# Long convolution with soft mixture of experts: x loaded in two blocks of 64 and 32 rows

## The chip, the cores and the metric

The kernel runs on one core of a Trainium2 chip. The metric is the device time of one execution in microseconds (us). TensorE is PE in the profile, VectorE DVE, ScalarE ACT, GpSimd POOL, and SyncE, which issues nearly all DMAs, SP.

## The reference, cut to what matters

`x` is (8, 5696, 128) and `h` is (5696, 128), both float32. Each of the 8 batches is convolved with `h` along its 5696 tokens, causally and per channel, by a transform of double length. The 45568 tokens that result go through a soft mixture of experts with 8 experts of 4 slots.

```python
Xf = np.fft.rfft(x, n=2*S, axis=1); Hf = np.fft.rfft(h, n=2*S, axis=0)
y = np.fft.irfft(Xf * Hf[None], n=2*S, axis=1)[:, :S, :]
t = y.reshape(B * S, D)
logits = t @ phi                       # 32 slots
slot_input = softmax(logits, over tokens).T @ t
slot_out = relu(slot_input @ w1) @ w2  # for each expert
out = softmax(logits, over slots) @ slot_out
```

## The kernel before, in words

The transform is a two-level one with N1 = 90 and N2 = 64. A sequence of 5696 tokens is seen as R1 = 89 rows of 64 tokens (5696 = 89 * 64; the transform along the rows yields 90 values). There are nine sequences ("batches" g): g = 0 is `h`, and g = 1 to 8 are the batches of `x`. A sequence is cut into NJ = 8 pieces of CH = 4 columns and their mirror images, so there are 72 steps t, one for each piece.

Stage A, once for each step. `load_x` brings piece c into one of three buffers `xc` of shape 128 partitions x 2 x 4 x 128: a row of x goes to a partition, and of each row two runs of 4 x 128 floats (2,048 bytes each) are taken, the piece and its mirror image. In the last piece of a sequence the two runs touch, and are one run of 4,096 bytes. `load_x(t + 3)` is called in step t, so a load is three steps ahead of its use. `fold` (L200, on POOL) adds and subtracts the two halves into `x0` and `x1`. `stage_a` multiplies them from the left by the table `s1` (L211, 128 x 128 weights, K = 128 partitions always), copies the bank to `fst` on ACT (L213) and stores the result in the DRAM tensor `f` by two DMAs of 45 partitions (L217), one from partition F0 = 6 and one from F1 = 82.

The 89 rows stand at partitions X0 = 20 to 108. They are loaded by two DMAs, rows 0 to 79 (SPLIT = 80) to partitions 20 to 99, and rows 80 to 88 to partitions 100 to 108. The remaining partitions of `xc` hold the zeros that a memset left there at the start, and the rows of `s1` that belong to them are zero too.

Stage B (`load_g` L230, `stage_b1` L244, `stage_b2` L284) reads `f` back in units of 128 partitions (`gt`, five buffers, asked for four units ahead), transforms along the other direction, multiplies by the transform of `h`, transforms back and stores in the DRAM tensor `z` (L289). It runs nine steps behind stage A, 23 units for each sequence. Stage C (`load_pair` L319, `stage_c1` to `stage_c6`) reads `z` back into `zc`, finishes the inverse transform and does the token side of the mixture of experts. Its load is already in the form that the change gives to x: 64 rows at partition 32 and 26 rows at partition 0, each row 16,384 bytes (`z_blocks`). There is such a pair of loads in every second step from t = 25 on.

The order of the program is written out by hand in the loop from L558. On SP's queue a step reads: the f stores and gt loads of the first half, `load_pair` (every second step), `load_x(t + 3)`, the two f stores of `stage_a(t, 1)`, a gt load, a z store. So the two x loads stand just behind the large `zc` loads, and just ahead of an f store and a gt load. All of them are in one queue. The last part of the program (from step 72) holds no x loads: the rest of stages B and C, the experts, and the output.

Of the kernel before, what the change touches and what calls it, by code (L numbers as in the profile page):

```python
# [17 lines left out]
def z_blocks(n):  # L18

    return [(0, 64, 32), (64, n - 64, 0)]  # L20


def transform_tables(S, N1, N2, CH, X0, F0, F1):

    N, R1, HALF, P = N1 * N2, S // N2, N2 // 2, 2 * N2
    k1 = np.arange(N1)
    alpha = np.pi * (k1 + 0.5) / N1
    m1 = np.arange(R1) - (N1 - 1) / 2
    a1 = np.outer(m1, alpha)  # L40
    s1 = np.stack([np.cos(a1), -np.sin(a1), -np.cos(a1)], 1)
    a0 = np.outer(alpha, np.arange(N1 // 2) + 0.5)
    i1 = np.stack([np.cos(a0), -np.sin(a0), -np.cos(a0)], 1)
    NP = N1 // 2
    part = s1
    s1 = np.zeros((P, 3, P))
    for a, p in enumerate((F0, F1)):
        s1[X0:X0 + R1, :, p:p + NP] = part[:, :, a * NP:(a + 1) * NP]
    part = i1[np.arange(N1).reshape(2, NP).T.reshape(-1)]
    i1 = np.zeros((P, 3, N2))  # L50
    for r, n, p in z_blocks(N1):
        i1[p:p + n, :, 0:NP] = part[r:r + n]
    k2 = np.arange(N2)
    omega = np.pi * (k1[:, None] + 2 * N1 * k2[None] + 0.5) / N
    m2 = np.arange(HALF) - (N2 - 1) / 2
    a2 = m2[None, :, None] * omega[:, None, :]
    w = np.concatenate([np.cos(a2), np.sin(a2)], 1)
    back = np.arange(N2).reshape(2, HALF // CH, CH).transpose(1, 0, 2).reshape(-1)
    NU = (NP + 1) // 2
    turn = (N1 - 1) / 2 * alpha[:, None] + (N2 - 1) / 2 * omega  # L60
    wq = np.zeros((2, N2, NP, N2))
    vq = np.zeros((2, N2, NU, 2, N2))
    tn = np.zeros((2, N2, 2, NU, 2))
    for a in range(2):
        wq[a] = w[a * NP:(a + 1) * NP].transpose(1, 0, 2)
        for q in range(NP):
            vq[q % 2, :, q // 2, a] = w[a * NP + q][back].T
            tn[q % 2, :, 0, q // 2, a] = np.cos(turn[a * NP + q]) / N
            tn[q % 2, :, 1, q // 2, a] = np.sin(turn[a * NP + q]) / N
    wq, vq, tn = [t.reshape(P, *t.shape[2:]) for t in (wq, vq, tn)]  # L70
    return [np.ascontiguousarray(t, dtype=np.float32) for t in (s1, i1, wq, vq, tn)]
# [3 lines left out]
def kernel(  # L75
# [26 lines left out]
    B, S, D = x.shape  # L102
# [4 lines left out]
    N1, N2 = 90, 64  # L107
    R1, HALF, NP = S // N2, N2 // 2, N1 // 2
    CH = 4
# [5 lines left out]
    HP = P // 2  # L115
    NQ = NJ // 2
    assert S == R1 * N2 and R1 == N1 - 1 and D == P and CH == Q == 4
    SPLIT = R1 // 16 * 16
    X0, F0, F1 = 20, 6, 82
    ctx.enter_context(tc.manual_schedule())  # L120

    t_s1, t_i1, t_w, t_v, t_turn = [
        nc.inline_tensor(t, f"tab_{n}").ap()
        for n, t in zip(("s1", "i1", "w", "v", "turn"), transform_tables(S, N1, N2, CH, X0, F0, F1))]
    fd = [nc.dram_tensor(f"f_{g}", (2, N2, NP, 2, D), F32, kind="Internal").ap() for g in range(B + 1)]
    zd = [nc.dram_tensor(f"z_{b}", (NP, 2 * N2, 2, D), F32, kind="Internal").ap() for b in range(B)]
    cd = nc.dram_tensor("c_t", (P, B * NQ, Q, 2, MH), F32, kind="Internal").ap()
# [7 lines left out]
    i1 = const.tile([P, 3, HP], F32, name="i1")  # L135
# [24 lines left out]
    s1 = apool.tile([P, 3, P], F32, name="s1", tag="s1", bufs=1)  # L160
    wt = fconst.tile([P, NP, HP], F32, name="wt")
    vt = fconst.tile([P, NU, 2, HP], F32, name="vt")
    turn = fconst.tile([P, 2, NU, 2], F32, name="turn")
# [3 lines left out]
    def bank():  # L167
        rings.append(rings.pop(0))
        return rings[-1].tile([P, 512], F32, name="bank", tag="bank")
# [8 lines left out]
    def load_x(c):  # L178
        if c >= (B + 1) * NJ:
            return  # L180
        g, j = divmod(c, NJ)
        src = (h if g == 0 else x[g - 1]).rearrange("(a n) d -> a n d", n=N2)
        t_ = xcs[c % len(xcs)]
        gap = N2 - CH * (2 * j + 1)
        for r in (slice(0, SPLIT), slice(SPLIT, R1)):
            v = src[r, CH * j:CH * (j + 1), :]
            v = bass.AP(tensor=v.tensor, offset=v.offset,
                        ap=[v.ap[0], [gap * D, 2], [1, CH * D]])
            nc.sync.dma_start(
                out=t_[X0 + r.start:X0 + r.stop, :, :, :].rearrange("p s n d -> p s (n d)"), in_=v)  # L190
        xs[c] = t_

    folded = {}
# [349 lines left out]
    loaded = 0  # L543

    load_x(0)
    nc.scalar.dma_start(out=s1[:, :, :], in_=t_s1)
    for c in range(1, 3):
        load_x(c)
# [9 lines left out]
    for t in range(last_front + 1):  # L558
# [73 lines left out]
        if t >= NA - 1:  # L632
# [6 lines left out]
            for r in (slice(N1 - 64, 32), slice(96, P)):  # L639
                nc.sync.dma_start(  # L640
                    out=zn[r, :, :, :, :, :].rearrange("k h o n c d -> k (h o n c d)"),
                    in_=zring[0][r, :, :, :, :, :].rearrange("k h o n c d -> k (h o n c d)"))
# [21 lines left out]
        if pair(-2) is not None:  # L664
            load_pair(pair(-2))
        load_x(t + 3)
        if t == NJ:
            prefetch(AHEAD)
# [38 lines left out]
    for q in range(Q):  # L707
        r = slice(q * NSL, (q + 1) * NSL)
        nc.gpsimd.tensor_copy(out=rep4[r, :, :],
                              in_=ident[r, r].unsqueeze(1).broadcast_to([NSL, Q, NSL]))  # L710
# [16 lines left out]
    for V in range(T, NT - 1):  # L727
# [33 lines left out]
        if V == T:  # L761
# [4 lines left out]
                              in_=moe_w1[E // 2:].rearrange("e d f -> d e f"))  # L766
        else:
            for i in range(4 * (V - T - 1), min(4 * (V - T), E), 2):
                nc.sync.dma_start(
                    out=w2s[:, i:i + 2, :, :],  # L770
                    in_=moe_w2[i:i + 2].rearrange("e (p c) d -> p e c d", p=P))
# [5 lines left out]
    p = bank()  # L777
# [8 lines left out]
    p = bank()  # L786
# [18 lines left out]
    for g in range(EG):  # L805
        for f0 in range(0, F, FH):
            p = bank()
# [4 lines left out]
            src = p[:, :].rearrange("p (c k) -> p k c", k=NFC)  # L812
# [4 lines left out]
    for g in range(EG):  # L817
        for k0 in range(0, NFC, 4):
            p = bank()
            for k in range(4):  # L820
# [3 lines left out]
                out=hidT[:, g, k0:k0 + 4, :], in_=p[:, :].rearrange("p (k c) -> p k c", k=4))  # L824
# [11 lines left out]
    p = bank()  # L836
# [20 lines left out]
    for b in range(B):  # L857
        first = [(0, 8), (8, 24)] if b == 0 else [(0, 32)]
        for r0, rows in first + [(32, 32), (64, 24)]:
# [3 lines left out]
            parts, at, r = [], 0, r0  # L863
            for n in (32, 16, 8):
                if rows & n:
                    parts.append((at, n * W // P, r))
                    at, r = at + n * W // P, r + n
# [14 lines left out]
            for q in range(Q):  # L882
                dst = ov4[:, 0:used + lone, q, :]
                src = pq[q][:, 0:(used + lone) * D].rearrange("p (k d) -> p k d", d=D)
# [4 lines left out]
            for at, n, r in parts:  # L889
                nc.sync.dma_start(  # L890
                    out=ov[b, r * N2:(r + n * P // W) * N2, :].rearrange(
                        "(p n) d -> p (n d)", p=P),
                    in_=o_[:, at * Q:(at + n) * Q, :].rearrange("p n d -> p (n d)"))
            if lone:
                nc.sync.dma_start(
                    out=ov[:, (R1 - 1) * N2:, :].rearrange("b (j n) d -> b j (n d)", n=CH),
                    in_=o_[:, used * Q:(used + 1) * Q, :].rearrange("p q d -> p (q d)"))
# [31 lines left out]
```

## Time and profile before

| what | value |
|---|---|
| median of 11 runs (range) | 925.08 us (920.18 to 935.58) |
| the profiled execution's own time | 926.8 us |
| its span, first to last instruction | 924.6 us |
| mean granted clock of TensorE | 0.961 |
| PE, DVE, ACT, POOL busy | 91%, 71%, 55%, 52% |
| DMA packets of SP's queue (q1), and MB | 164,795, 271.39 MB |
| x loads (with those of h) | 72 of 320 KB and 72 of 36 KB |
| zc loads | 28 of 1,024 KB and 28 of 416 KB |

Busy times are shares of the span. "DMA share" is the mean busy share of the core's 16 DMA engines. In the list of waits a line reads: who waited, for whom, us in total, how often, the longest. In the chain and the timeline a line begins with its start and its length in us.

### The profile page before, as it was taken

The numbers are of one execution on the slowest core, as the hardware profiler recorded it, in microseconds if no ns is written. First come the engines' busy times: TensorE is split into PE (matmuls) and PEld (weight loads), VectorE is DVE, ScalarE is ACT, GpSimd is POOL, SyncE is SP. The second block draws the span as 40 slices with busy tenths as digits, with TensorE's granted clock in tenths as the row PEclk, the third lists the DMA queues.
The fourth block names the chain that finished last, engine by engine and source line by source line (L and its number), as shares of the span: only waits on it lengthen the run. The fifth ranks groups of instructions, "written<-read, shape, count | busy, mean of one in ns | idle before, by whom it ended". The sixth has DMA issues, their size and how long they took to land.

```text
span 924.6 us, 20380 instructions
## 1 busy us (share of the span) xinstructions
PE 837.6 (91%) x7220; PEld 402.6 (44%) x7220; DVE 656.3 (71%) x1119; ACT 512.0 (55%) x1018; POOL 476.7 (52%) x437
## 2 busy tenths in 40 slices
PE   6968888889999999999999999999998888897994
PEld 2323233334444444444444444444443334354894
DVE  3035576678888887887788788878886888786443
ACT  3546545446666665665565656565664454676442
POOL 4647623335565555555455555555545567575300
PEclk9989999999999999999999999999998999998955
DMA  8889899999999999999999999999998788885897
GB/s 287 268 269 279 267 286 330 295 322 307 313 301 315 298 298 296 329 307 275 306 277 300 296 304 299 293 297 303 323 334 249 244 282 268 256 292 186 322 419 321
DMA packets 165471, 273.04 MB, mean 295 GB/s; under 512 B 14886, under 2 KB 117542, under 8 KB 160277
## 3 DMA queue, kind: packets, MB, share of 16 engines
q1 hardware_dynamic: 164795, 271.39, 91.7%
q8 instruction: 58, 0.95, 0.4%
q10 hardware_dynamic: 576, 0.36, 0.2%
q14 instruction: 42, 0.34, 0.1%
HBM read 142.85 MB, written 128.21 MB: 293 GB/s over the span
## 4 chain that ended last, share of the span: by engine, by line
PE 63%; DMA 20%; DVE 4%; ACT 4%; POOL 3%; issue 3%; SPq 2%; DVEq 0%; ACTq 0%; POOLq 0%
PE bank L211 19%; PE bank L336 11%; PE bt L244 11%; DMA gt<-f 9%; PE bz L284 7%; DMA f<-fst 6%; DMA out_dram<-o 3%; PE bank L370 3%; PE bank L455 2%; PE op L873 2%; PE bank L379 2%; PE bank L408 2%; POOL y L360 2%; PE bank L431 2%; ACT fst L213 1%
## 5 line engine op out<-in xcount | busy, mean ns | idle before, releaser
L211 PE MATMUL bank<-x,s 128*128 128x512 f32 x576 | 284.1, 620 | 10.8 <-POOL x L200 8.3
L200 POOL TENSOR_TENSOR x<-xc 128x512 f32<-128x512 f32 x144 | 183.4, 1275 | 146.8 <-PE bank L211 98.2
L213 ACT ACTIVATE fst<-bank 128x512 f32<-128x512 f32 x288 | 167.6, 596 | 96.8 <-PE bank L211 67.0
L265 DVE TENSOR_TENSOR pr<-bt,Hr 128x512 f32<-128x512 f32 (+1 forms) x184 | 126.9, 689 | 108.5 <-PE bt L244 98.1
L288 ACT ACTIVATE zst<-bz 128x512 f32<-128x512 f32 (+1 forms) x184 | 108.2, 588 | 149.9 <-PE bz L284 143.3
L244 PE MATMUL bt<-gt,wt 64*64 64x256 f32 x1620 | 138.8, 406 | 47.8 <-DMA gt<-f 21.3
L211 PEld LDWEIGHTS bank<-x,s 128*128 128x128 f32 x576 | 99.8, 192 | 133.6 <-issue 88.5
L270 DVE TENSOR_TENSOR yf<-pr,pi 128x512 f32<-128x512 f32 (+1 forms) x166 | 145.1, 874 | 5.7
L268 DVE TENSOR_TENSOR pi<-bt,Hi 128x512 f32<-128x512 f32 (+1 forms) x184 | 125.0, 680 | 0.0
L284 PE MATMUL bz<-yf,vt 64*64 64x256 f32 x1440 | 116.2, 382 | 2.0 <-DVE yf L270 0.6
L244 PEld LDWEIGHTS bt<-gt,wt 64*64 64x64 f32 x1620 | 45.4, 133 | 164.7 <-PE bank L211 41.7
L336 PE MATMUL bank<-zc,i 128*64 128x512 f32 x448 | 110.9, 618 | 0.0
L360 POOL TENSOR_TENSOR y<-y,op 128x512 f32<-128x512 f32 x64 | 77.4, 1210 | 58.9 <-DVE op L341 56.3
L360 POOL TENSOR_TENSOR y<-y,om 128x512 f32<-128x512 f32 x59 | 82.1, 1391 | 2.1
L284 PEld LDWEIGHTS bz<-yf,vt 64*64 64x64 f32 x1440 | 52.6, 132 | 38.3 <-issue 12.7
L255 DVE SCALAR_TENSOR_TENSOR Hr<-bt,turn,ph 128x128 f32<-128x128 f32 (+1 forms) x46 | 16.0, 349 | 69.7 <-ACT ph L253 69.7
L370 PE MATMUL bank<-ident,y 109*128 109x109 f32 x512 | 57.2, 262 | 3.0 <-POOL y L360 3.0
L372 ACT ACTIVATE yt<-bank 128x360 f32<-128x360 f32 x128 | 52.1, 473 | 12.5 <-PE bank L370 12.4
L370 PEld LDWEIGHTS bank<-ident,y 109*128 109x128 f32 x512 | 48.6, 141 | 18.2 <-issue 11.6
L444 POOL TENSOR_TENSOR L<-L,rs 128x512 f32<-128x512 f32 x32 | 43.0, 1344 | 16.6 <-DVE rs L443 13.0
L873 PE MATMUL op<-so,cT 32*128 32x128 f32 x704 | 48.5, 413 | 2.8 <-ACT o L888 2.2
L336 PEld LDWEIGHTS bank<-zc,i 128*64 128x64 f32 x448 | 27.9, 139 | 50.5 <-issue 45.4
(100 smaller groups left out, 867.1 us busy)
## 6 DMA issues: line engine op xcount, KB each, us to landing
f<-fst SPq DMA_DIRECT2D x288, 180.0 KB
gt<-f SPq DMA_DIRECT2D x198, 256.0 KB
z<-zst SPq DMA_DIRECT2D x176, 256.0 KB
zc<-z SPq DMA_DIRECT2D x28, 1024.0 KB
xc<-in_x_dram SPq DMA_DIRECT2D x64, 320.0 KB
out_dram<-o SPq DMA_DIRECT2D x15, 1024.0 KB
zc<-z SPq DMA_DIRECT2D x28, 416.0 KB
out_dram<-o SPq DMA_DIRECT2D x9, 512.0 KB
```

Of the source, the lines that this page charges most:

```text
L200: nc.gpsimd.tensor_tensor(out=y_[:, :, :], in0=t_[:, 0, :, :], in1=t_[:, 1, ::-1, :], op=AL.subtract if comp else AL.add)
L211: nc.tensor.matmul(p[:, :], s1[:, tab[G], :], src[:, :, :].rearrange("p n d -> p (n d)"), start=True, stop=True)
L213: nc.scalar.activation(st[:, :, G, :], p[:, :].rearrange("p (n d) -> p n d", d=D), AF.Copy)
L244: nc.tensor.matmul(bt[q * HP:(q + 1) * HP, a, 0:2 * D], wt[r, 2 * i + q, :], t_[r, q, :, :].rearrange("p c d -> p (c d)"), start=True, sto ...
L265: nc.vector.tensor_tensor(out=pr[r, :, :, :], in0=pv, in1=Hr[r, i, :, :].unsqueeze(2).broadcast_to([n * HP, 2, 2, D]), op=AL.mult)
L268: nc.vector.tensor_tensor(out=pi[r, :, :, :], in0=pv, in1=Hi[r, i, :, :, :], op=AL.mult)
L270: adder.tensor_tensor(out=y_[r, :, :, :], in0=pr[r, :, :, :], in1=pi[r, :, ::-1, :], op=AL.add)
L284: nc.tensor.matmul(bz[a * HP:(a + 1) * HP, q, 0:2 * D], vt[r, i, a, :], y_[r, a, :, :].rearrange("p c d -> p (c d)"), start=True, stop=True)
L288: nc.scalar.activation(st[:, 0:n, :], bz[:, 0:n, 0:2 * D], AF.Copy)
L336: nc.tensor.matmul(p[h_ * HP:(h_ + 1) * HP, :], i1[:, tab, :], t_[:, h_, o, :, q, :], start=True, stop=True)
L360: eng.tensor_tensor(out=part(v, f), in0=part(v, 0), in1=o_[:, :, :], op=sign)
L370: nc.tensor.transpose(p[:, i * TR:(i + 1) * TR], ys[T][0:TR, k * CH + i, 0:D], ident[0:TR, 0:TR])
```

## The change

The 89 rows are loaded as rows 0 to 63 to partitions 32 to 95, and rows 57 to 88 to partitions 0 to 31. Rows 57 to 63 are thus loaded twice. The table `s1` gets its rows at the same places: rows 0 to 63 at partition 32, rows 64 to 88 at partitions 7 to 31, and zeros at partitions 0 to 6, where the repeated rows lie, and at 96 to 127. Nothing else in the program is different: the number of instructions, their order on each engine and their shapes are the same but for the shapes of the x loads.

```diff
+def x_blocks(n):
+    return [(0, 64, 32), (n - 32, 32, 0)]
...
     for a, p in enumerate((F0, F1)):
-        s1[X0:X0 + R1, :, p:p + NP] = part[:, :, a * NP:(a + 1) * NP]
+        done = 0
+        for r, n, row in x_blocks(R1):
+            s1[row + done - r:row + n, :, p:p + NP] = part[done:r + n, :, a * NP:(a + 1) * NP]
+            done = r + n
...
-    SPLIT = R1 // 16 * 16
-    X0, F0, F1 = 20, 6, 82
+    F0, F1 = 6, 82
...
-        for r in (slice(0, SPLIT), slice(SPLIT, R1)):
-            v = src[r, CH * j:CH * (j + 1), :]
+        for r, n, p in x_blocks(R1):
+            v = src[r:r + n, CH * j:CH * (j + 1), :]
             v = bass.AP(tensor=v.tensor, offset=v.offset,
                         ap=[v.ap[0], [gap * D, 2], [1, CH * D]])
             nc.sync.dma_start(
-                out=t_[X0 + r.start:X0 + r.stop, :, :, :].rearrange("p s n d -> p s (n d)"), in_=v)
+                out=t_[p:p + n, :, :, :].rearrange("p s n d -> p s (n d)"), in_=v)
```

More of the change, by code (lines that the diff above doesn't have):

```diff
@@ L20, in z_blocks, with transform_tables @@
     return [(0, 64, 32), (64, n - 64, 0)]
-def transform_tables(S, N1, N2, CH, X0, F0, F1):
+def x_blocks(n):
+    return [(0, 64, 32), (n - 32, 32, 0)]
+def transform_tables(S, N1, N2, CH, F0, F1):
     N, R1, HALF, P = N1 * N2, S // N2, N2 // 2, 2 * N2
@@ L123 @@
         nc.inline_tensor(t, f"tab_{n}").ap()
-        for n, t in zip(("s1", "i1", "w", "v", "turn"), transform_tables(S, N1, N2, CH, X0, F0, F1))]
+        for n, t in zip(("s1", "i1", "w", "v", "turn"), transform_tables(S, N1, N2, CH, F0, F1))]
     fd = [nc.dram_tensor(f"f_{g}", (2, N2, NP, 2, D), F32, kind="Internal").ap() for g in range(B + 1)]
```

## The prediction

> **What bounds the kernel now.** I read the page first, for the busy shares and the chain.
>
> ```profile
> PE 837.6 (91%) x7220; PEld 402.6 (44%) x7220; DVE 656.3 (71%) x1119; ACT 512.0 (55%) x1018; POOL 476.7 (52%) x437
> ...
> q1 hardware_dynamic: 164795, 271.39, 91.7%
> ...
> PE 63%; DMA 20%; DVE 4%; ACT 4%; POOL 3%; issue 3%; SPq 2%; DVEq 0%; ACTq 0%; POOLq 0%
> ```
>
> PE and the 16 DMA engines are both busy for 91% or more, so a change to the DMAs alone could matter or vanish. The split by stage decides (columns: PE, PEld, DVE, ACT, POOL busy, granted clock, DMA share, GB/s):
>
> ```profile
> 45.00:185.00 140.00, 114.48 (x737) 42.94 (x736) 79.78 (x171) 74.09 (x146) 64.46 (x60) 0.96 0.93 287
> 185.00:700.00 515.00, 501.94 (x4260) 231.34 (x4260) 420.32 (x680) 309.00 (x598) 284.03 (x245) 1.00 0.97 303
> ```
>
> From 185 to 700 us, where 44 of the 72 x loads fall (the first at 181.8), PE is idle for 13.1 of 515 us although DMA has 97%. Whatever DMA gains there, the end cannot gain over 13.1 us; a loss has no such cap. Then the waits of that stretch, PE's and SP's, and POOL's waits for x over the whole run:
>
> ```profile
> PE bt L244 <- DMA gt<-f: 11.5, 8, 2.5
> ...
> SPq L217 <- DMA zc<-z: 98.8, 39, 5.0
> SPq L230 <- DMA f<-fst: 18.0, 6, 4.4
> ...
> SPq L230 <- DMA xc<-in_x_dram: 9.8, 24, 0.8
> ```
> ```profile
>   DMA xc<-in_x_dram: 6.5, 4
> ```
>
> x itself is hardly waited for: fold L200 lost 6.5 us in four waits, being fed three steps ahead. (SP's waits for zc and x come from its eight DMA semaphores, used in turn: a ninth DMA waits until the first has landed.) PE waits for gt, in eight places. One of them, by the chain and then by PE's timeline:
>
> ```profile
> 336.79 8.62 DMA f<-fst
> ...
> 345.49 2.84 DMA gt<-f
> ```
> ```profile
> 348.38 0.66 PE L244 MATMUL bt<-gt,wt 64*64 64x256 f32 x8 [0.59 <-DMA gt<-f]
> ```
>
> An f store that usually lands 4.5 us after its issue (its median, from the semaphore updates) took 8.6, and the gt load behind it 2.8; other matmuls covered all but 0.59 us. The stretch before it shows why it was late:
>
> ```profile
> 337.00:338.00 1.00, 1.00 (x22) 0.51 (x24) 1.00 (x2) 0.74 (x2) 1.00 (x2) 1.00 0.88 344
> ...
> 339.00:340.00 1.00, 1.00 (x17) 0.61 (x10) 0.94 (x4) 0.33 (x1) 1.00 (x2) 1.00 0.70 139
> 340.00:341.00 1.00, 1.00 (x14) 1.00 (x13) 0.96 (x2) 1.00 (x4) 1.00 (x1) 1.00 0.73 141
> 341.00:342.00 1.00, 1.00 (x13) 0.81 (x15) 0.74 (x1) 1.00 (x4) 1.00 (x2) 1.00 1.06 260
> ```
>
> A `zc` pair was issued at 333.5 us, x behind it at 334.7. While the 64-row zc block moves, the rate is 344 GB/s; when the 26-row block at partition 0 and x move, it falls to 140. The packet records say the same: 16 KB packets that begin in the fourth microsecond after the issue took 687 ns on average, in the sixth and seventh 1,200; 2,048-byte packets there took 164 to 173 ns against a median of 84 over the run. Of the x loads, 22 stand behind a zc pair; their 80-row DMA lands 9.8 us after issue (median), in the other steps 4.9.
>
> **The change part by part.**
>
> *Instructions.* SP issues two x DMAs a step before and after, in the same place (their issue takes 0.42 us each, median). Nothing passes another queue, no wait is added, and POOL, PE, ACT and DVE run the same instructions on 128 partitions: `s1` has K = 128 either way, and the zeros are weights. Cost: 0.
>
> *Rows on a DMA engine.* How many engines a DMA uses is seen in the semaphore updates that it leaves: 16 for the 80 rows, ten for the nine rows (nine engines and one step of the issuer), and the 4-byte completion packets in q1 (14,566) are what the largest divisor of the row count up to 16 gives for every DMA. So nine engines carried 5 + 1 rows, seven carried 5; after, 64 and 32 rows make 4 + 2 on all. The fullest engine has 12 packets of 2,048 bytes in both: 12 x 84 ns = 1.01 us. The seven lighter ones gain two packets, 0.17 us. That the fullest engines end a load is visible: the nine-row DMA lands 0.18 to 0.20 us (two packets) after the 80-row one in 47 of 61 pairs. In the other 14 a lighter engine is last, and there the pair may come up to 0.17 us later, in a load that is three steps early. Cost on the path: 0.
>
> *Bytes.* Seven more rows are 28,672 bytes a load, 72 loads: q1 should show 2.06 MB more (273.5), 0.76%. At the stage's 303 GB/s that is 0.095 us a load, at the 141 GB/s of the slow stretch 0.203. All 72 loads fully exposed would be 6.8 us at the first rate. But only eight gt waits in this stretch reach PE. In them, with x ahead in the queue at the slow rate: 8 x 0.203 = 1.6 us. In the other steps it is hidden by PE's own work; without that cover the 22 slow loads cost 4.5 us. From 45 to 185 us PE idles 25.5 us, but 7.7 us of that is gt, in three waits, while the f and x loads run beside no zc load: up to 3 x 0.095 = 0.3, which I leave out.
>
> *Placement.* No row shows a 64-row x load at partition 32 or a 32-row one at partition 0; the nearest are the two zc blocks at the same partitions. Good end: x in 64 rows moves as the 64-row zc block does, at full speed even there. Ten packets at 160 ns become eight at 84 (-0.93 us), two at 160 become four (+0.32): -0.6 us. Bad end: the 32 rows go as the 26-row block does. 128 KB at 140 GB/s is 0.94 us where 36 KB took 0.26 (+0.68), less 64 KB at 340 GB/s (-0.19): +0.5 us. Outside the slow stretches x packets take 94 to 99 ns on average beside 84, so there is nothing to win, and any loss has PE's cover. Between -0.6 and +0.5 I take 0: each block is nearest to its own zc row, and the two ends nearly cancel.
>
> [...]
>
> *Sum.* The profiled execution took 926.8 us (span 924.6), 1.7 above the median of 925.1. From the median: 925.1 + 1.6 = 926.7.
>
> **The rivals.**
>
> *Slower: the low block becomes the bottleneck.* 16 engines write 32 low partitions just behind 13 engines that write 26 of the same. The bad end, 0.5 us plus 0.2 for the bytes, in 8 stretches (5.6) to 22 (15, if every slow stretch then reaches PE): 931 to 940, likeliest 932. For it: the 140 GB/s rows. Against it: the fullest engine has no more rows. It decides from 0.58 us a place on in eight places, or 0.21 in 22 (4.6 us).
>
> *Faster: x was slow through its own placement.* 0.6 us less in 8 stretches (-4.8), and SP's 9.8 us of waiting for x to land before it issues gt shrink as well; the cap is the 11.5 us that PE waits there for gt: 914 to 920, likeliest 919. For it: the 80 rows straddle both halves of the partitions, and rate falls when they move. Against it: in 39 loads without a zc pair ahead the same 80 rows run at 94 to 99 ns.
>
> *The rows aren't the matter:* the waits of 9.8 us behind zc are zc's own 1,440 KB, and x, at 356 KB, moves nothing. That is my forecast without the 1.6 us: 925.
>
> **How the numbers follow.** A measurement of this kernel can tell about 0.5% (4.6 us) from no change. Forecast (925 to 928, with or without the bytes): 0.41. Slower rival: 0.38, since loss has no cap and three things point there (bytes, low partitions, seven engines more at work). Faster rival: 0.21, since it needs more than a third of all PE idleness of the stage. The forecast's own range is 921 to 929.7. For 8 in 10 the range reaches to 917 and 936, leaving out the far end of each rival.
>
> **What would show it.** q1 with 273.5 MB and about 1,450 packets more (945 of data, 504 of completion) shows the bytes and the 16 engines. The gt wait of PE from 185 to 700 us tells the cases apart: 11 to 14 us for the forecast, over 16 for the slower rival, under 7 for the faster. In the slow stretches the mean of the 2,048-byte packets should stay at 150 to 170 ns; near 100 it is the faster rival, near 200 the slower. PE's busy time in that stage should stay within 1 us of 501.9. I am wrong altogether if the time moves without PE's gt wait moving: then the granted clock or the first 185 us did it.

## The result and the profile after

The changed kernel takes 935.06 us (median of 12 runs, 925.27 to 941.14) against 925.22 for the kernel before in the same measurement: ratio 1.0117, 95% interval 1.0086 to 1.0147. It is 1.2% slower. (Ratios, here and below, are over the runs within 1.5% of the fastest of their kernel, so they differ a little from those of the medians.) A second measurement of the same kernel gave 1.0073 (1.0031 to 1.0114), and the mean of the two is 0.95%. The forecast was no change (926.7 us); the time fell into the part of the range that belonged to the rival "the low block becomes the bottleneck" (931 to 940). The profiled execution took 933.14 us, span 931.0, mean granted clock 0.959.

The page of the changed kernel, the lines that answer to those shown first:

```profile
PE 840.5 (90%) x7220; PEld 403.2 (43%) x7220; DVE 656.0 (70%) x1119; ACT 512.2 (55%) x1018; POOL 476.7 (51%) x437
...
q1 hardware_dynamic: 166244, 273.45, 91.2%
...
PE 65%; DMA 20%; DVE 3%; ACT 3%; issue 3%; POOL 3%; SPq 2%; DVEq 0%; ACTq 0%; POOLq 0%
```

q1 moved 2.06 MB and 1,449 packets more, as predicted, 945 of them data and 504 completion packets of 4 bytes, seven for each of the 72 loads: the seven rows and the 16 engines are there. The engines do the same work. The stretches of time (columns as before):

```profile
45.00:185.00 140.00, 113.90 (x701) 42.00 (x700) 76.58 (x167) 71.78 (x140) 63.43 (x58) 0.94 0.91 282
185.00:700.00 515.00, 504.56 (x4271) 232.19 (x4269) 420.93 (x681) 310.51 (x601) 283.98 (x244) 1.00 0.98 307
```

The first of these stretches is where this execution falls behind: 701 matmuls get done in it, where the kernel before does 737, and the granted clock is 0.94 where it was 0.96. Step 24 (of the 72 steps t) begins 5.2 us late on PE, before and after:

```profile
165.68 1.98 PE L211 MATMUL bank<-x,s 128*128 128x512 f32 x4
```
```profile
170.88 1.98 PE L219 MATMUL bank<-x,s 128*128 128x512 f32 x4
```

From 185 to 700 us PE is even a little busier in this execution. Its wait for gt there, and three of SP's waits:

```profile
PE bt L252 <- DMA gt<-f: 8.8, 8, 2.3
...
SPq L225 <- DMA zc<-z: 87.7, 38, 4.7
SPq L238 <- DMA f<-fst: 18.7, 8, 3.8
...
SPq L238 <- DMA xc<-in_x_dram: 4.9, 13, 0.7
```

PE's wait went from 11.5 to 8.8 us, the wrong way for a slower kernel; in the second measurement's profile the same line reads 15.4 us. One execution cannot carry a difference of 1%. The stalls of a few us that decide it fall in other places each time. The beginnings of the steps show this too (taken at a step's first copy to `fst`): behind the kernel before, the changed one is late by 3.8 us at step 12, by 8.1 at step 47, by 3.0 at step 71 and by 6.4 at the end. From here on, ratios of many runs decide, and a trace is read for what recurs, in every step or in many kernels' traces.

One duration recurs in every step. These are the x loads on SP, of the kernel before and of the changed one (minimum, median and maximum of the issue in ns, first and last start):

```profile
L189 SPq DMA_DIRECT2D xc<-in_x_dram x128: 283/423/1569, 35.2 to 668.5; - x128
L189 SPq DMA_DIRECT2D xc<-in_h_dram x16: 313/392/1200, 2.0 to 31.9; - x16
```
```profile
L197 SPq DMA_DIRECT2D xc<-in_x_dram x128: 328/597/1807, 36.0 to 672.9; - x128
L197 SPq DMA_DIRECT2D xc<-in_h_dram x16: 561/592/765, 2.0 to 32.6; - x16
```

The instructions are the same in number and place, but an issue takes 0.60 us where it took 0.42. It shows in the first microseconds, when nothing else is queued: six issues take 4.00 us instead of 2.87 (start and length in us, SP's timeline before and after).

```profile
1.97 2.87 SPq L189 DMA_DIRECT2D xc<-in_h_dram  x6
```
```profile
1.97 4.00 SPq L197 DMA_DIRECT2D xc<-in_h_dram  x6
```

Summed over the records of the traces, the issues of x and h hold SP for 69.0 us before and 96.7 after: 0.958 and 1.344 us a step, 27.7 us more in all. The second measurement's profile has 99.3.

Three theories were put to the test. **A**: the loss is SP's time, because f stores and gt loads stand behind the x pair. **B**: the loss is the seven rows' bytes, or the seven engines more. **C**: the loss is the 32 rows in the lowest partitions, where zc's 26 rows land just before. A fourth, **S**, puts it in the start-up, where the issues come thick.

### The profile page after: what moved, and what is told of

The parts are those of the page before. It is cut to its first block, busy times and chain, and to the rows that moved or that the text cites. A ratio compares the mean times of both kernels' runs of the same rounds, so it can differ in the third digit from the quotient of the medians.

```text
span 931.0 us, 20380 instructions
## 1 busy us (share of the span) xinstructions
PE 840.5 (90%) x7220; PEld 403.2 (43%) x7220; DVE 656.0 (70%) x1119; ACT 512.2 (55%) x1018; POOL 476.7 (51%) x437
## 3 DMA queue, kind: packets, MB, share of 16 engines
q1 hardware_dynamic: 166244, 273.45, 91.2%
## 4 chain that ended last, share of the span: by engine, by line
PE 65%; DMA 20%; DVE 3%; ACT 3%; issue 3%; POOL 3%; SPq 2%; DVEq 0%; ACTq 0%; POOLq 0%
PE bank L219 20%; PE bank L344 12%; PE bt L252 11%; DMA gt<-f 8%; PE bz L292 8%; DMA f<-fst 7%; PE bank L378 3%; DMA out_dram<-o 3%; PE bank L463 2%; PE op L881 2%; PE bank L416 2%; PE bank L387 2%; PE bank L439 2%; POOL y L368 1%; ACT fst L221 1%
```

## The experiments

Ratios are to the kernel before, with the 95% interval. "x on SP" is the sum of all issues of x and h in the profiled execution; the kernel before has 69.0 us, the changed one 96.7.

### Other blocks, one property at a time

Each of these four is the changed kernel with one line different, the table following it.

**Sixteen engines and seven rows more, the old first block** (`e1_16rows`):

```diff
-    return [(0, 64, 32), (n - 32, 32, 0)]
+    return [(0, 80, 20), (n - 16, 16, 100)]
```

> Rows 0 to 79 at partitions 20 to 99 as before; the second load is 16 rows (73 to 88) at partitions 100 to 115, its seven repeated rows under zeros. The same bytes and the same 16 engines as the changed kernel, without its blocks. Theory A (issue: each x DMA holds SP 0.60 us instead of 0.42, 36 us more on SP in all): the first load's issue goes back to 0.43 us, so at most half of the 1.2%, +0.0 to +0.6%. Theory B (seven more rows and seven more engines at work): the whole +1.2%, as in the changed kernel. Theory C (32 low partitions behind the 26-row zc block): 0.0%.

Measured: 1.0059 (1.0023 to 1.0094), x on SP 74.9 us.

**The second block at partition 96** (`e2_high`, run again as `e2b_high`):

```diff
-    return [(0, 64, 32), (n - 32, 32, 0)]
+    return [(0, 64, 32), (n - 32, 32, 96)]
```

> As the changed kernel, but the 32-row block stands at partitions 96 to 127 instead of 0 to 31. Theory A: +1.2%, with x issues still at 0.60 us. Theory B: +1.2%. Theory C: back to 0.0%, and in the stretches behind a zc pair the 2,048-byte packets get shorter than in the changed kernel.

> The kernel with the 32-row block at partitions 96 to 127 again, beside the changed kernel on the same chip. Theory C (half of the loss is the low block): 0.5% under the changed kernel. Theories A and B: the same as the changed kernel within 0.3%.

Measured: 1.0060 (1.0020 to 1.0099) and 1.0039 (1.0009 to 1.0070), x on SP 101.9 and 95.9 us. The issues stay long without a low block, and roughly half of the loss remains.

**No repeated rows** (`e3_25rows`):

```diff
-    return [(0, 64, 32), (n - 32, 32, 0)]
+    return [(0, 64, 32), (64, n - 64, 7)]
```

> 64 rows at partition 32 as in the changed kernel, but then only the 25 rows that are left, at partitions 7 to 31: no repeated row, five engines for the second load (five rows each). Theory A: if the 0.60 us belong to the 64 rows or the low partitions, the issues stay long and the time stays up by 0.6 to 1.2%. Theory B: bytes are back to those of before, so about 0.0%, unless nine rows on five engines (18 packets, 1.5 us) make those the last to land. Theory C: 25 low partitions instead of 32, so +0.9%.

Measured: 1.0127 (1.0071 to 1.0183), x on SP 86.5 us; q1 is back at 271.38 MB. The bytes are gone, and the loss isn't.

**Twenty-three repeated rows, an 80-row block** (`e4_bytes`):

```diff
-    return [(0, 64, 32), (n - 32, 32, 0)]
+    return [(0, 80, 16), (n - 32, 32, 96)]
```

> Rows 0 to 79 at partitions 16 to 95, then 32 rows (57 to 88) at partitions 96 to 127, 23 of them repeated under zeros: 23 more rows than before where the changed kernel has seven, at no low block. Theory B: 3.3 times the loss, about +3.9%. Theory A: as the 16-row kernel, +0.0 to +0.6%. Theory C: 0.0%.

Measured: 1.0114 (1.0040 to 1.0189), x on SP 72.4 us. Theory B wanted three times the loss for three times the bytes. It did not come. There is some loss without SP time, which may be the bytes; the ratio rests on three runs.

The clean test of B came later: **two blocks of 48 rows** (`t48_two_halves`), with the same seven repeated rows, all 16 engines and the same 273.45 MB in q1, but short issues and nothing below partition 32.

```diff
-    return [(0, 64, 32), (n - 32, 32, 0)]
+    return [(0, 48, 32), (n - 48, 48, 80)]
```

> Rows 0 to 47 at partitions 32 to 79 and rows 41 to 88 at 80 to 127: seven repeated rows and 16 engines as in the changed kernel, two equal DMAs, no block in partitions 0 to 31. If the issue of 0.60 us belongs to blocks of 64 and 32 rows and goes back to 0.42 here: theory A 0.0%, theory B +0.6% as the 16-row kernel. If it stays at 0.60: A +1.2%.

Measured: 1.0009 (0.9980 to 1.0037), x on SP 74.1 us. In this layout seven rows and seven engines cost nothing that can be measured. Against `e2_high` (1.0060 and 1.0039) the rows repeated, the engines and the empty low partitions are the same, and the length of the issue is the main thing that differs.

### Where in the run

**The new layout for x alone** (`s1_x_only`) **and for h alone** (`s2_h_only`), each layout with a table of its own:

```diff
+OLD = [(0, 80, 20), (80, 9, 100)]
+NEW = [(0, 64, 32), (57, 32, 0)]
+H_BLOCKS, X_BLOCKS = OLD, NEW    # s2_h_only: NEW, OLD
...
-            nc.tensor.matmul(p[:, :], s1[:, tab[G], :],
+            nc.tensor.matmul(p[:, :], (s1x if g else s1)[:, tab[G], :],
```

> The change for the 64 loads of x alone; the eight loads of h keep their 80 and 9 rows, with a second table s1x for x. Theory S (the loss is made in the first ten steps, where SP's issues set the pace and x is h): 0.0 to +0.4%, and step 12 begins within 1 us of before (74.2 us). Theory B (bytes and engines) and theory C (low block behind zc), both of the steady stage: 64 of 72 loads, so +1.0 to +1.2%.

> The change for the eight loads of h alone; x keeps 80 and 9 rows. Theory S: +0.4 to +0.8% of the 1.2%, step 12 begins 3 to 4 us after the 74.2 us of before. Theories B and C: +0.1% or less.

Measured: x alone 1.0080 (1.0047 to 1.0113), h alone 1.0009 (0.9962 to 1.0055). In the traces, step 12 begins at 74.2 us before, 78.0 in the changed kernel, 76.2 and 75.9 in these two. The start-up is late in all of them, but h's eight loads are not the loss: it comes with x's 64.

Twenty of these 64 fall before 185 us, and there the traces, those below too, point one way. Nine of them add SP time by long x issues or by waits (the changed kernel twice, `s1_x_only`, `e2_high`, `e2b_high`, `e3_25rows`, and from below `f2_zhigh_after`, `d3_spdose`, `d1_sp_delay`): PE begins step 24 later than in the kernel before by 3.5 us on average (-0.9 to 6.1). Seven have short issues (`e1_16rows`, `e4_bytes`, `s2_h_only`, `c1_one_dma`, `c2_best`, `c3_one_low`, `f1_zhigh_before`): 0.2 us (-1.9 to 1.7). So a part of the loss is made before the first zc load (180.5 us). The clock is lower there too: up to 185 us it was granted at 0.5 for 17.1 us in both traces of the changed kernel and in `s1_x_only`, and for 10.2 us before. Whether the lower clock comes from the delays or adds to them is not shown.

### SP's time by itself

**The kernel before, x issued from ScalarE's queue** (`a1_act_queue`):

```diff
-            nc.sync.dma_start(
+            nc.scalar.dma_start(
```

> The kernel before with its x and h loads issued from ScalarE's queue instead of SP's; layout and bytes as before. Theory S: SP has 0.8 us less to issue in each of the first ten steps, where its issues take 4.1 us a step and PE needs 3.8, so step 12 begins 2 to 3 us earlier, -0.2 to -0.4%. Theories B and C: 0.0%, or slower by what ScalarE loses (0.8 us a step, half hidden).

Measured: 1.0738 (1.0681 to 1.0795). That takes the issues off SP and loses 7.4%. From 185 to 700 us ScalarE's copies to `fst`, now in one queue with the x issues, wait 35.3 us for f stores in place of 10.3, and PE's wait for gt rises to 43.4 us. It says nothing about A, since the place of the issues among ScalarE's work changed with the queue.

```profile
PE bt L244 <- DMA gt<-f: 43.4, 14, 6.9
```

**The kernel before with SP time added** (`d1_sp_delay`, and a third of it in `d3_spdose`): waits that are met already, ahead of each x pair. (The expectation of `d3_spdose` says behind the pair; they stand ahead of it.)

```diff
+    idle = nc.alloc_semaphore("idle")
...
+        for i in range(44):              # d3_spdose: 18
+            nc.sync.wait_ge(idle, 0)
```

> The kernel before, with 22 idle instructions of SP ahead of each pair of x loads (waits on a semaphore that are met already, 17 ns each in the trace of before, so some 0.37 us a step): SP's time is dosed as the changed kernel's longer issues dose it (0.39 us a step), with layout, bytes and number of DMAs as before. Theory A (SP's time): +0.6 to +1.2%. Theories B (bytes, engines) and C (low block): 0.0%.

> The kernel before, its layout of x untouched, with 18 waits that are already met put on SP behind each pair of x DMAs (nine or ten EVENT_SEMAPHOREs some 0.06 us apart, 0.55 us, less about 0.17 us that the x DMAs' own issues shrink when they stand apart): some 0.39 us of SP time more per step, the same as the changed kernel adds. Theory A (the loss is SP's issue time): +0.9 to +1.3%. Theory C (half of the loss is the low block of 32 rows at partition 0, and the issue time gives only what the layout at 64 and 96 gave): +0.3 to +0.6%. If an SP delay of this size is absorbed: within 0.3%.

Measured: `d1_sp_delay` 1.0346 (1.0308 to 1.0384), `d3_spdose` 1.0077 (1.0035 to 1.0119). What was added is read from the chain of waits of `d1_sp_delay` in the start-up:

```profile
46.96 0.03 SPq L184
46.99 0.03 issue
47.02 0.03 SPq L184
...
47.93 0.32 SPq L193
48.26 0.05 issue
48.31 3.14 DMA xc<-in_x_dram
```

Two waits share an instruction, and each instruction takes 0.06 us with the gap behind it: 22 a step are 1.33 us, 9 a step 0.54. The x issues themselves shrink (344 and 348 ns median, from 423), so x and waits together hold SP for 2.12 and 1.37 us a step instead of 0.958. That is 83.7 us more for 32.0 us of time (0.38 per us) and 29.9 us more for 7.1 us (0.24 per us). `d3_spdose` gives SP about what the changed kernel gives it (29.9 against 27.7 us), without touching layout, bytes or engines, and the kernel is 0.8% slower. In `d1_sp_delay` PE's wait for gt shows where it ends; with `d3_spdose` (second line) it is no longer than before (11.5):

```profile
PE bt L248 <- DMA gt<-f: 29.3, 15, 5.6
```
```profile
PE bt L248 <- DMA gt<-f: 11.7, 11, 3.2
```

Most of the added time vanishes where SP would have waited anyhow: all its waits over 0.15 us sum to 462 us before, 431 with `d3_spdose`, 397 with `d1_sp_delay` and 430 in the changed kernel. Only a part of that is the wait for zc to land before the f stores, from 185 to 700 us: 98.8 us before, then 94.7, 84.0 and 87.7.

### SP's time taken away

**One x DMA of 96 rows**, the seven rows more being the next batch's: in `c1_one_dma` for batches 1 to 7 at partition 20, in `c2_best` for all eight at partition 32, where h's two loads begin too (the last batch begins seven rows earlier and has its own table).

```diff
+        whole = g > 0                    # c1_one_dma: 0 < g < B
+        if whole:
+            r0 = (g - 1) * R1 - (96 - R1 if g == B else 0)
+            src = x.rearrange("b (a n) d -> (b a) n d", n=N2)[r0:r0 + 96, :, :]
...
-        for r in (slice(0, SPLIT), slice(SPLIT, R1)):
+        for r in ([slice(0, 96)] if whole else (slice(0, SPLIT), slice(SPLIT, R1))):
```

> Layout of before, but for the first seven batches of x one DMA of 96 rows to partitions 20 to 115 (six rows an engine) instead of 80 and 9; the seven rows beyond the batch are the next batch's, under zeros. The same bytes as the changed kernel in 56 of 72 loads, 16 engines, no low block, 56 issues fewer on SP (24 us of issue). Theory B: +0.4 to +0.6%, as the 16-row kernel. Theory A (issue on SP): -0.3 to -0.6%. Theory S: 0.0%, since h is as before.

> The kernel before with one x DMA of 96 rows at partition 32 for all eight batches of x (the last batch begins seven rows earlier, with a table of its own), h as before. Theory A: SP gets back some 0.55 us per step in all eight batches, a little more than the kernel with one DMA for seven of them: -0.5 to -0.9%. Theory B (repeated rows and the bytes cost the time): +0.5 to +1.0%.

Measured: 0.9943 (0.9909 to 0.9977) and 0.9917 (0.9879 to 0.9955), x on SP 38.0 and 33.0 us. Both beat the kernel before, with the same seven rows more in nearly every load. `c2_best` gets 35.9 us of SP back and 7.7 us of time: 0.21 per us, close to what `d3_spdose` lost. This is not a pure dose of SP time: with one DMA less a step, SP also waits for other older DMAs (its eight DMA semaphores are used in turn: in the kernel before, 958 of 959 of its DMAs take the semaphore of the eighth ahead of them; it waits for zc 78.8 us in place of 102.3, from 185 to 700 us), and no run separates the two. The x loads of `c2_best`, and PE's wait for gt from 185 to 700 us:

```profile
L197 SPq DMA_DIRECT2D xc<-in_x_dram x64: 332/406/877, 35.5 to 658.0; - x64
```
```profile
PE bt L252 <- DMA gt<-f: 3.9, 4, 1.5
```

### The low block

**The z block moved off the low partitions**, in the kernel before (`f1_zhigh_before`) and in the changed one (`f2_zhigh_after`):

```diff
-    return [(0, 64, 32), (64, n - 64, 0)]
+    return [(0, 64, 32), (64, n - 64, 96)]
...
-            for r in (slice(N1 - 64, 32), slice(96, P)):
+            for r in (slice(0, 32), slice(96 + N1 - 64, P)):
```

> The kernel before with the 26-row block of the z load moved from partition 0 to partition 96, so that nothing of z lies in the lowest partitions. It is the partner of the next run. Theory A: 0 to +0.3% (the z block is only moved). Theory C: 0 to -0.3% (the 9 low rows of x lose a neighbour).

> The changed kernel with the same move of the z block. Theory A: over its partner by what the changed kernel is over the kernel before, +0.9 to +1.3%. Theory C (x's 32 low rows and z's 26 low rows crowd the same partitions): over its partner by half of that, +0.3 to +0.6%.

Measured: 1.0069 (1.0026 to 1.0113) and 1.0130 (1.0086 to 1.0174). Their difference, 0.6%, lies at the upper edge of C and under the lower edge of A, so it decides nothing. And the first of them, expected to be harmless, lost 0.7% on its own, which no theory here explains.

**One DMA at partitions 0 to 95** (`c3_one_low`): `c2_best` with 32 low rows behind the zc pair and the same single issue.

```diff
-    X0, F0, F1 = 32, 6, 82
+    X0, F0, F1 = 0, 6, 82
```

> The kernel with one DMA of 96 rows for all eight batches, at partitions 0 to 95 instead of 32 to 127, the same partitions as the changed kernel fills, 32 of them low, in the same loads just behind z. Theory A (only SP's issue time counts): -0.5 to -0.9% against the kernel before, as with the rows at partition 32. Theory C (32 rows at the low partitions cost by themselves): some 0.4 to 0.5% less gain than that, -0.4 to 0%.

Measured: 0.9960 (0.9923 to 0.9997), 0.4% less gain than `c2_best` and at the low end of what C expected; x on SP 35.7 us. The two intervals overlap (0.9960 plus or minus 0.0037, 0.9917 plus or minus 0.0038). The traces lean the same way: behind a zc pair, x lands 10.63 us after its issue (median of the 22 loads) in place of 9.63, the 2,048-byte packets of the next 8 us take 154 ns in place of 137, and PE waits longer for gt. But that wait alone differed as much between two traces of the changed kernel (8.8 and 15.4):

```profile
PE bt L252 <- DMA gt<-f: 11.4, 12, 2.0
```

The changed kernel and its twin at partition 96 (`e2_high`, `e2b_high`) differ by as much: 0.95% against 0.50%, each the mean of two measurements. Their traces do not put this behind the zc pairs: there the x pair lands after 9.70 and 10.25 us in the changed kernel and after 10.13 and 10.20 in the twin, and at step 24, before any zc load, the changed kernel is already 5.2 and 6.1 us late and the twin -0.9 and 3.8. The second measurement of the changed kernel:

> The changed kernel again, for the comparison with the high block: +1.2% by its first measurement.

Measured: 1.0073 (1.0031 to 1.0114), x on SP 99.3 us.

### The issue time by itself

`m1_issue` does not compute anything: SP issues x loads of twenty combinations of row count and first partition, eight times each, then five kinds of pairs, and zeros are stored to the output.

```python
ONE = [(9, 100), (16, 100), (24, 64), (32, 0), (32, 96), (40, 32), (48, 32), (48, 80), (56, 32),
       (64, 0), (64, 20), (64, 32), (72, 32), (80, 20), (88, 20), (89, 20), (96, 0), (96, 32),
       (112, 0), (128, 0)]
PAIRS = [((80, 20), (9, 100)), ((64, 32), (32, 0)), ((48, 32), (48, 80)), ((80, 32), (32, 0)),
         ((64, 32), (16, 0))]
```

> Not the computation: SP issues loads of x alone, eight in a row for each of twenty pairs of row count and first partition, each row two runs of 2,048 bytes, then five sets of pairs, then zeros are stored to the output. It measures the disputed cost, the issue time of an x DMA by its rows, with little else in the queue. If the issue time follows the row count as in the kernels: near 0.6 us for 64 and 32 rows, 0.4 to 0.5 for 80, 48 and 16, whatever the first partition. If it came from what else was queued in the kernel: all alike.

Measured, on SP's timeline (start, length in us). The numbers in the names count the loads, two for each. First 32 rows at partition 0; 64 rows at partitions 0, 20 and 32; 80 rows:

```profile
13.79 0.31 SPq L49 DMA_DIRECT2D r_p__114<-in_x_dram  x1
...
56.96 0.60 SPq L49 DMA_DIRECT2D r_p__218<-in_x_dram  x1
...
65.25 0.58 SPq L49 DMA_DIRECT2D r_p__230<-in_x_dram  x1
...
75.21 0.58 SPq L49 DMA_DIRECT2D r_p__246<-in_x_dram  x1
...
88.41 0.31 SPq L49 DMA_DIRECT2D r_p__274<-in_x_dram  x1
```

Then the pair 80 and 9 of the kernel before, the pair 64 and 32 of the changed one, and 64 and 16:

```profile
277.45 0.31 SPq L49 DMA_DIRECT2D pair80and_r__386<-in_x_dram  x1
279.46 0.28 SPq L49 DMA_DIRECT2D pair80and_r__388<-in_x_dram  x1
...
289.18 0.59 SPq L49 DMA_DIRECT2D pair64and_r__406<-in_x_dram  x1
289.81 0.59 SPq L49 DMA_DIRECT2D pair64and_r__408<-in_x_dram  x1
...
304.06 0.59 SPq L49 DMA_DIRECT2D pair64and_r__446<-in_x_dram  x1
304.69 0.59 SPq L49 DMA_DIRECT2D pair64and_r__448<-in_x_dram  x1
```

A DMA of 64 rows holds SP for 0.58 to 0.60 us at each of its three first partitions, and the smaller one after it does the same. By themselves 32 and 16 rows take 0.31 us, as do 80 rows, and 32 rows that follow 80. All other counts from 9 to 112 but one (89) settle at 0.28 to 0.32. So the long issue belongs to the 64-row shape. The expectation, that 32 rows are slow by themselves, was wrong; they are slow behind 64.

## Why the prediction was wrong, point by point

**The step that failed: "Instructions", "Cost: 0".** It took the issue time of the kernel before (0.42 us) for the new DMAs because their number and place stayed. The issue takes 0.60 us, and 27.7 us more of SP are worth, at the 0.24 of `d3_spdose`, 6.7 us or 0.7%. The twin at partition 96, with issues as long, lost 0.5%. The trace of before had a warning: its zc pair, blocks of 64 and 26 rows at the partitions of the new x blocks, took 0.51 and 0.55 us to issue (medians) where the x pair took 0.44 and 0.40. I used the zc rows to bound the placement and not to bound the issue; they would have given 0.22 us a step, 16 us of SP. That SP's time passes to the end is shown by adding it (`d1_sp_delay` far beyond the noise, `d3_spdose` at the size in question); taking it away (`c1_one_dma`, `c2_best`) agrees. No rival of mine held this mechanism; the slow rival got the right time mostly for the wrong reason.

**Rows on a DMA engine** and **bytes:** right. q1 has the 16 engines and the bytes, and `t48_two_halves` shows both together at +0.1% (my 1.6 us were 0.2%). The landings were read too narrowly: the nine-row DMA of x lands last in 48 of 64 pairs, by 0.01 to 0.36 us, with a median of 0.20.

**Placement**, "Between -0.6 and +0.5 I take 0": this may have been too low. `c3_one_low` against `c2_best` says about 0.4%, 4 us, the changed kernel against its twin at partition 96 the same, and 4 us over the 22 slow stretches would be 0.2 us each, inside the bounds. It is not shown: the first difference is within its uncertainty, the second barely outside. The changed kernel's traces do not show it either: behind a zc pair x lands after 9.70 and 10.25 us where it was 9.95, and the 2,048-byte packets take 143 and 149 ns where they took 144.

**The sum as the runs leave it:** 0.5 (the twin) to 0.8% (`d3_spdose`) from SP's issue time, and perhaps 0.4% from the low block, make 0.5 to 1.2%, against 1.2 and 0.7% measured. That SP's time costs this much is shown, within the limits named below. The low block's part is open.

**The marks:** q1's packets and bytes were right. PE's busy time from 185 to 700 us, to stay within 1 us of 501.9, was 504.6 and 498.0 in two profiles of the same changed kernel, so it tells nothing at this size. PE's gt wait was a bad mark too: 8.8 and 15.4 us. It separates large effects (3.9 in `c2_best`, 29.3 in `d1_sp_delay`, 43.4 in `a1_act_queue`) and not 1%. "I am wrong altogether if the time moves without PE's gt wait moving: then the granted clock or the first 185 us did it" came out half true. The mean clock is 0.959 and 0.961, and the loads of h alone (`s2_h_only`) are worth 0.1%; but 5.2 and 6.1 us of lateness stand at step 24 in the two traces of the changed kernel, within the first 185 us, with a lower clock there. The forecast weighed the x loads of that stretch by their bytes (0.3 us, left out) and not by their issues.

**What stays open:** why a 64-row DMA takes twice as long to issue (0.58 to 0.60 us against 0.28 to 0.32), and the one behind it as long. And `e1_16rows`, `e4_bytes` and `f1_zhigh_before` lost 0.6 to 1.1% with 6 us or less of SP time added; bytes may explain the second, nothing that was run explains the other two. `e1_16rows` has the rows, engines and SP time of `t48_two_halves`, which lost nothing. Layout effects of half a per cent are thus near the limit of what these runs can assign, and the size of SP's part is no surer than that.

## What to carry to other kernels

Where one queue issues nearly everything, price a new DMA shape by its issue time too, and take that time from a measurement of the shape, not from the DMA that it replaces. A microsecond of issue ahead of loads that PE needs cost 0.2 to 0.4 us here where time was added by itself, and one DMA with seven useless rows beat two exact ones (-0.8%). When a change is worth 1%, look in the trace for a duration that repeats every step, and leave the verdict on stalls to medians.

## What the runs showed of the hardware

- In `m1_issue` the issue time on SP does not follow the size: 9 to 112 rows of two 2,048-byte runs settle at 0.28 to 0.32 us but for 64 and 89 rows, 128 rows take 0.37, and 64 rows 0.58 to 0.60.
- 89 rows in one DMA took far longer there. The seven issues after the first take 12.8 to 14.7 us each:

```profile
110.37 12.84 SPq L49 DMA_DIRECT2D r_p__304<-in_x_dram  x1
123.25 14.07 SPq L49 DMA_DIRECT2D r_p__306<-in_x_dram  x1
```

  88 rows take 0.29 us. Each 89-row DMA leaves two semaphore updates, where an 88-row one leaves 12, and the first of these DMAs lands after 22.8 us, where 88 rows take 10.0 to 10.6. The trace of the kernel before shows how such counts can be read: the 14,566 completion packets of q1 are the sum, over its DMAs, of the largest divisor of the row count up to 16, and a nine-row DMA leaves one update 0.46 to 1.47 us after its issue begins (the issuer's) and nine more, none before 2.34 us. Read so, the 12 updates are 11 engines and one step of the issuer, and the two are one engine and that step, since 89 is prime. That one engine moved all 89 rows is an estimate from these counts.
- Waits that are met already cost SP 0.06 us where two share an instruction, the gap behind it included (`d1_sp_delay`).
- Moving the x issues to ScalarE's queue cost 7.4% (`a1_act_queue`), though SP was relieved of them.
